# The second token tile's output projection: three fp32r matmuls on high and low parts instead of one fp32 matmul

## The chip, the cores and the metric

One core of a Trainium2 chip. The metric is the device time of one execution in microseconds, the median of three runs. The engines are TensorE (PE, with PEld for its weight loads), VectorE (DVE), ScalarE (ACT), GpSimd (POOL) and SyncE (SP), which issues the DMAs.

## The reference

Attention with keys and values pooled by 8, then two gated feed-forward layers over 2304 tokens, all fp32:

```python
# 4 batches, 8 heads, 576 tokens, head dimension 64: 2304 tokens of 512 columns
attn = softmax(scale * q @ mean8(k).T);  x = attn @ mean8(v)
# first layer, 512 -> 1536 -> 512
xn = x / rms * rms_g
g = xn @ w_gate
silu = g * (1.0 / (1.0 + np.exp(-g)))
val = xn @ w_val
x = silu * val @ w_out
# second layer, 512 -> 1536 -> 512
return (x @ w_a) * (x @ w_b) @ w_out2
```

## The kernel before

The first layer works on five tiles of tokens, `TILES1 = [512, 256, 512, 512, 512]` (line 20); the change concerns the second one, `idx == 1`, which has 256 tokens. The attention of later tokens is computed beside the matmuls of a tile: while tile 1 runs, the sub-tiles 6 to 9 of 128 tokens each pass through it, as the list `SIDE` (line 630) hands out their steps (`sub_steps`, line 287): scores (`sc`), maximum, exponent (`E`), transposition (`eP`, `eT`), values (`av`), normalization (`x`), sum of squares (`sq`, `ss`), a root per pair of sub-tiles (`root`, line 420, lines 427 to 441: `ba`, `br` and `by`, tensors of 128x2), the scaling of x (line 398) and its transposition (`xP`, line 405), from which the next tile's input is split into `xh` and `xl`.

For each of the twelve blocks f of 128 hidden columns a tile does this (loop from line 1106): gate and value projections (`project`, line 545), each 4 chunks x 3 matmuls, because an fp32 product is made of fp32r matmuls (a shortened fp32 format): low weights by high x, high by high, high by low. The parts of the weights are made anew for each tile by `split_w` (line 533): `wh` by a ScalarE cast, `wl` by a GpSimd subtraction, two buffers of each, so a block's parts are made when those of two blocks before are released. SiLU on ScalarE (line 1120) gives `ht`, VectorE multiplies it by the value (line 1127). Then the output projection of the block before it is added into four accumulators. In tiles 2 to 4 that is `out_proj` (line 562), 12 fp32r matmuls from `hh` and `hl`, the two parts of `ht` (lines 1136, 1137), and from `wh2` and `wl2`. In tiles 0 and 1 it is `out_direct` (line 573), 4 matmuls on fp32 `ht` and fp32 weights; the program issues each as two, so the profile shows 8 records per block. In tile 1 `ht` changes between two buffers, in tiles 2 to 4 it has one.

Tile 0 and all from the last tile on are ordered by hand. Tiles 1 to 3 are ordered by a scheduler when the program is built; each engine then works through its own list in that order, and an instruction that waits holds up all behind it on its engine.

Of the kernel before, what the change touches and what calls it, by code (L numbers as in the profile page):

```python
# [8 lines left out]
F32 = mybir.dt.float32  # L9
F32R = mybir.dt.float32r  # L10
# [7 lines left out]
P = 128  # L18
# [44 lines left out]
def attention_moe_moe2(  # L63
# [42 lines left out]
    h_p = first.enter_context(tc.tile_pool(name="h", bufs=2))  # L106
# [426 lines left out]
    def split_w(ph, f, i, part=None):  # L533
        if part != 1:
            wh = ws_p.tile([P, KD, P], F32R, tag=f"wh{i}", name=f"wh{i}")
            wl = ws_p.tile([P, KD, P], F32R, tag=f"wl{i}", name=f"wl{i}")
            nc.scalar.copy(wh, wf[ph, f, i])  # L537
            ws[i, f] = (wh, wl)
        if part != 0:
            wh, wl = ws[i, f]  # L540
            (nc.vector if boot["alt"] else nc.gpsimd).tensor_sub(  # L541
                wl, wf[ph, f, i], wh.bitcast(F32)
            )

    def project(tag, f, part, xs, cols, last, mid=None):
        xh, xl = xs
        wh, wl = ws.pop((part, f)) if last else ws[part, f]
        bank = ps.tile([P, 512], F32, tag=tag, name=tag)
        n = cols.stop - cols.start
        i = 0  # L550
        for c in range(KD):
            if c == 2 and mid is not None:
                mid()
            for w, x in ((wl, xh), (wh, xh), (wh, xl)):
                nc.tensor.matmul(  # L555
                    bank[:, :n], w[:, c, :], x[:, c, cols],
                    start=(i == 0), stop=(i == 3 * KD - 1),
                )
                i += 1
        return bank  # L560

    def out_proj(ph, f, accs, hs, cols, last):
        hh, hl = hs
        wh, wl = ws.pop((2, f)) if last else ws[2, f]
        n = cols.stop - cols.start
        for c in range(KD):
            for i, (w, x) in enumerate(((wl, hh), (wh, hh), (wh, hl))):
                nc.tensor.matmul(  # L568
                    accs[c][:, cols], w[:, c, :], x[:, :n],
                    start=(f == 0 and i == 0 and cols.start == 0), stop=(f == NF - 1 and i == 2),  # L570
                )

    def out_direct(f, accs, ht, cols):

        for c in range(KD):
            nc.tensor.matmul(  # L576
                accs[c][:, cols], wf[0, f, 2][:, c, :], ht[:, :cols.stop - cols.start],
                start=(f == 0 and cols.start == 0), stop=(f == NF - 1),
            )
# [65 lines left out]
    def new_accs():  # L645
        pairs = [ps.tile([P, 2, 512], F32, tag=f"acc{i}", name=f"acc{i}") for i in range(2)]
        return [pairs[c // 2][:, c % 2] for c in range(KD)]
# [432 lines left out]
    for idx, (ph, t0, n) in enumerate(work):  # L1080
        last_tile = idx + 1 == len(work)
        nxt = None if last_tile else work[idx + 1]
        side = SIDE[idx] if idx < len(SIDE) else []
        region = ExitStack()
        if last_tile:
            attn.close()
            side = second_front()
        if last_tile or idx == 0:
            region.enter_context(tc.manual_schedule(engines=set(HELD)))
        full = slice(0, n)  # L1090
        jobs = [(f, full, True, f + 1, True) for f in range(NF)]
        slot = {"n": 0, "done": 0}
        total = 4 * len(jobs)

        def step():
            slot["n"] += 1
            want = -(-len(side) * slot["n"] // total)
            while slot["done"] < want:
                side[slot["done"]]()
                slot["done"] += 1  # L1100

        accs = first_tile() if idx == 0 else new_accs()
        if idx == 0:
            jobs = []
        prev = None
        for f, cols, last, ahead, own in jobs:
            m = cols.stop - cols.start
            if ahead == NF:
                ahead = None if nxt is None else (nxt[0], 0)
            elif ahead is not None:  # L1110
                ahead = (ph, ahead)
            gb = project("g", f, 0, xs, cols, last)
            if ahead is not None:
                split_w(*ahead, 0)
            step()
            if idx == 1:
                ht = h_p.tile([P, 512], F32R, tag=("hh", "hl")[f % 2], name="ht").bitcast(F32)
            else:
                ht = h_p.tile([P, 512], F32, tag="ht", name="ht", bufs=1)
            nc.scalar.activation(out=ht[:, :m], in_=gb[:, :m], func=AF.Silu)  # L1120
            vb = project("v", f, 1, xs, cols, last, step)
            if ahead is not None:
                split_w(*ahead, 1)
            if own and idx > 1:
                split_w(ph, f, 2)
            step()
            nc.vector.tensor_mul(ht[:, :m], ht[:, :m], vb[:, :m])  # L1127
            if idx == 1:
                if prev is not None:
                    out_direct(prev[0], accs, *prev[1:3])  # L1130
                step()
                prev = (f, ht, cols, last)
                continue
            hh = h_p.tile([P, 512], F32R, tag="hh", name="hh")
            hl = h_p.tile([P, 512], F32R, tag="hl", name="hl")
            nc.scalar.copy(hh[:, :m], ht[:, :m])
            nc.vector.tensor_sub(hl[:, :m], ht[:, :m], hh.bitcast(F32)[:, :m])
            if prev is not None:
                out_proj(ph, prev[0], accs, *prev[1:])
            step()  # L1140
            prev = (f, (hh, hl), cols, last)
        if prev is not None and idx == 1:
            out_direct(prev[0], accs, *prev[1:3])
        elif prev is not None:
            out_proj(ph, prev[0], accs, *prev[1:])
        if nxt is not None:
            xs = XT[idx + 1]
        for c, acc in enumerate(accs):
            if last_tile:
                if c == 0:  # L1150
                    last_x = x_p.tile([P, KD, 512], F32R, tag="xh", name="last_x").bitcast(F32)
                ev = last_x[:, c]
            else:
                ev = ev_p.tile([P, 512], F32, tag="ev", name="ev")
            if c % 2 == 0:
                nc.scalar.copy(ev[:, :n], acc[:, :n])
            else:
                nc.vector.tensor_copy(ev[:, :n], acc[:, :n])
            nc.sync.dma_start(out=x2d[t0][c * P:(c + 1) * P, :], in_=ev[:, :n])
        region.close()  # L1160
# [60 lines left out]
```

## Time and profile before

| | |
|---|---|
| median of 3 runs | 994.43 us (994.41 to 997.38) |
| profiled execution | 994.85 us, span 992.9 us |
| busy: TensorE, VectorE, ScalarE, GpSimd | 960.8 (97%), 533.3 (54%), 448.2 (45%), 347.7 (35%) us |
| mean granted TensorE clock | 0.997 |
| tile 1 on TensorE | 169.10 to 243.21 us |

The span is the time from the first to the last instruction. Matmuls are pipelined: a record of a matmul is longer than its step to the next one, so lengths of work are taken from start to start. The granted clock is 1.00 at 2.4 GHz and 0.50 at 1.2 GHz.

### The profile page before, as it was taken

How to read it: one execution, taken by the hardware profiler on the slowest of the kernel's cores; microseconds unless marked ns; L12 is line 12 of the kernel's file. 1: busy time of each engine (PE TensorE's matmuls, PEld its weight loads, DVE VectorE, ACT ScalarE, POOL GpSimd, SP SyncE). 2: the span in 40 equal slices, each digit the busy share in tenths (PEclk: the TensorE clock that was granted, in tenths of full speed). 3: DMA queues.
4: the chain of work that ended last, by engine and by line, in shares of the span. 5: the costliest groups of instructions: out<-in, count | busy, mean ns of one | idle time of the engine just before them, and what ended most of it. 6: DMA issues, size and time to landing. Idle time of an engine off the chain costs nothing. (4 is left out here: it accounts for less than half of the span.)

```text
span 992.9 us, 13291 instructions
## 1 busy us (share of the span) xinstructions
PE 960.8 (97%) x4866; PEld 831.8 (84%) x4866; DVE 533.3 (54%) x875; ACT 448.2 (45%) x800; POOL 347.7 (35%) x293
## 2 busy tenths in 40 slices
PE   5889889999999999999999999999999999999998
PEld 4776556898888888888888899999999999888886
DVE  5799876433442424242158588777666665222321
ACT  4667353654635455453355455444343444321211
POOL 3424512443343444343475603344433333310000
PEclk9999999999999999999999999999999999999999
DMA  8565662000000010000120242444434435643431
GB/s 288 184 230 172 212 204 88 22 23 22 22 1 22 1 54 1 1 1 2 49 93 7 85 162 97 143 138 144 130 130 126 157 111 213 192 150 105 143 110 66
DMA packets 47776, 101.79 MB, mean 103 GB/s; under 512 B 5216, under 2 KB 19808, under 8 KB 47712
## 3 DMA queue, kind: packets, MB, share of 16 engines
q1 hardware_dynamic: 47568, 100.82, 31.2%
q8 instruction: 39, 0.64, 0.3%
q14 instruction: 25, 0.20, 0.1%
q10 hardware_dynamic: 144, 0.13, 0.0%
HBM read 74.19 MB, written 26.74 MB: 102 GB/s over the span
## 5 line engine op out<-in xcount | busy, mean ns | idle before, releaser
L541 POOL TENSOR_TENSOR wl<-wf,wh 128x512 fp32r<-128x512 f32 x142 | 189.4, 1341 | 269.9 <-ACT wh L537 266.4
L537 ACT CAST wh<-wf 128x512 fp32r<-128x512 f32 x156 | 94.5, 617 | 68.8 <-PE v L555 38.5
L1001 PE MATMUL o<-woh,hl 128*128 128x512 f32 x216 | 85.8, 397 | 0.0
L979 DVE TENSOR_TENSOR hl<-hf,hh 128x768 fp32r<-128x768 f32 x36 | 35.3, 986 | 93.5 <-ACT hh L978 93.4
L1001 PE MATMUL o<-woh,hh 128*128 128x512 f32 x216 | 85.0, 394 | 0.0
L1001 PE MATMUL o<-wol,hh 128*128 128x512 f32 x216 | 84.7, 392 | 0.0
L1127 DVE TENSOR_TENSOR ht<-ht,v 128x512 f32<-128x512 f32 (+1 forms) x48 | 29.6, 617 | 92.9 <-PE v L555 84.7
L555 PE MATMUL g<-xh,wl 128*128 128x512 f32 (+1 forms) x192 | 72.7, 379 | 0.0
L555 PE MATMUL v<-xh,wl 128*128 128x512 f32 (+1 forms) x192 | 71.9, 375 | 0.0
L555 PE MATMUL v<-xl,wh 128*128 128x512 f32 (+1 forms) x192 | 70.0, 364 | 0.0
L555 PE MATMUL v<-xh,wh 128*128 128x512 f32 (+1 forms) x192 | 69.9, 364 | 0.0
L555 PE MATMUL g<-xl,wh 128*128 128x512 f32 (+1 forms) x192 | 69.9, 364 | 0.0
L555 PE MATMUL g<-xh,wh 128*128 128x512 f32 (+1 forms) x192 | 69.7, 363 | 0.0
L576 PE MATMUL acc<-ht,wf 128*128 128x256 f32 (+1 forms) x208 | 69.4, 475 | 0.0
L978 ACT CAST hh<-hf 128x768 fp32r<-128x768 f32 x36 | 29.8, 834 | 87.2 <-PE o L1001 79.4
L513 POOL TENSOR_TENSOR w<-w,st 128x512 int32<-128x512 int32 x20 | 26.2, 1311 | 114.0 <-DVE w L506 112.9
L908 ACT COPY p<-X 128x384 f32<-128x384 f32 x36 | 17.3, 480 | 89.5 <-PE X L900 89.5
L568 PE MATMUL acc<-hh,wl 128*128 128x512 f32 x144 | 56.7, 394 | 0.0
L568 PE MATMUL acc<-hl,wh 128*128 128x512 f32 x144 | 56.4, 391 | 0.0
L568 PE MATMUL acc<-hh,wh 128*128 128x512 f32 x144 | 56.1, 389 | 0.0
L576 PEld LDWEIGHTS acc<-ht,wf 128*128 128x128 f32 x208 | 39.8, 198 | 19.0 <-issue 15.3
L1120 ACT ACTIVATE ht<-g 128x512 f32<-128x512 f32 (+1 forms) x48 | 26.1, 544 | 57.9 <-PE g L555 57.8
(197 smaller groups left out, 2511.6 us busy)
## 6 DMA issues: line engine op xcount, KB each, us to landing
hf<-h SPq DMA_DIRECT2D x36, 384.0 KB, 3.2
st<-in_moe_w_out_dram SPq DMA_DIRECT2D x24, 512.0 KB, 3.7
h<-u SPq DMA_DIRECT2D x36, 192.0 KB, 2.3
h<-p SPq DMA_DIRECT2D x36, 192.0 KB, 1.9
st<-in_moe_w_gate_dram SPq DMA_DIRECT2D x12, 512.0 KB, 3.7
st<-in_moe_w_val_dram SPq DMA_DIRECT2D x12, 512.0 KB, 4.1
st<-in_moe_w_a_dram SPq DMA_DIRECT2D x12, 512.0 KB, 4.4
st<-in_moe_w_b_dram SPq DMA_DIRECT2D x12, 512.0 KB, 3.4
```

The costliest lines, as they stand in the source:

```text
L513: (nc.vector if boot["alt"] else nc.gpsimd).tensor_tensor(out=bits, in0=bits, in1=low, op=ALU.add)
L537: nc.scalar.copy(wh, wf[ph, f, i])
L541: (nc.vector if boot["alt"] else nc.gpsimd).tensor_sub(wl, wf[ph, f, i], wh.bitcast(F32))
L555: nc.tensor.matmul(bank[:, :n], w[:, c, :], x[:, c, cols], start=(i == 0), stop=(i == 3 * KD - 1),)
L568: nc.tensor.matmul(accs[c][:, cols], w[:, c, :], x[:, :n], start=(f == 0 and i == 0 and cols.start == 0), stop=(f == NF - 1 and i == 2),)
L576: nc.tensor.matmul(accs[c][:, cols], wf[0, f, 2][:, c, :], ht[:, :cols.stop - cols.start], start=(f == 0 and cols.start == 0), stop=(f == ...
L908: nc.scalar.copy(t, src[:, :HALF])
L978: nc.scalar.copy(hh, hf)
L979: nc.vector.tensor_sub(hl, hf, hh.bitcast(F32))
L1001: nc.tensor.matmul(accs[i], x[:, sub], y, start=(f == 0 and j == 0), stop=(f == NF - 1 and j == 2),)
L1120: nc.scalar.activation(out=ht[:, :m], in_=gb[:, :m], func=AF.Silu)
L1127: nc.vector.tensor_mul(ht[:, :m], ht[:, :m], vb[:, :m])
```

## The change

Tile 1 is now treated as tiles 2 to 4: `ht` has one buffer, `split_w(ph, f, 2)` makes `wh2` and `wl2` for each block, a ScalarE cast makes `hh`, a VectorE subtraction `hl`, and `out_proj` does 12 fp32r matmuls of 256 columns where `out_direct` did 4 fp32 ones.

```diff
--- before.py
+++ after.py
@@ -1113,24 +1113,15 @@
             if ahead is not None:
                 split_w(*ahead, 0)
             step()
-            if idx == 1:
-                ht = h_p.tile([P, 512], F32R, tag=("hh", "hl")[f % 2], name="ht").bitcast(F32)
-            else:
-                ht = h_p.tile([P, 512], F32, tag="ht", name="ht", bufs=1)
+            ht = h_p.tile([P, 512], F32, tag="ht", name="ht", bufs=1)
             nc.scalar.activation(out=ht[:, :m], in_=gb[:, :m], func=AF.Silu)
             vb = project("v", f, 1, xs, cols, last, step)
             if ahead is not None:
                 split_w(*ahead, 1)
-            if own and idx > 1:
+            if own:
                 split_w(ph, f, 2)
             step()
             nc.vector.tensor_mul(ht[:, :m], ht[:, :m], vb[:, :m])
-            if idx == 1:
-                if prev is not None:
-                    out_direct(prev[0], accs, *prev[1:3])
-                step()
-                prev = (f, ht, cols, last)
-                continue
             hh = h_p.tile([P, 512], F32R, tag="hh", name="hh")
             hl = h_p.tile([P, 512], F32R, tag="hl", name="hl")
             nc.scalar.copy(hh[:, :m], ht[:, :m])
@@ -1139,9 +1130,7 @@
                 out_proj(ph, prev[0], accs, *prev[1:])
             step()
             prev = (f, (hh, hl), cols, last)
-        if prev is not None and idx == 1:
-            out_direct(prev[0], accs, *prev[1:3])
-        elif prev is not None:
+        if prev is not None:
             out_proj(ph, prev[0], accs, *prev[1:])
         if nxt is not None:
             xs = XT[idx + 1]
```

The scheduler orders all five engines anew within tile 1. Three places follow, all around the root of the first pair of sub-tiles (6 and 7), whose `x_6` and `x_7` are transposed in tile 1 for tile 2. `ht`, `hh` and `hl` carry a running number, `wl0`, `wl1` and `wl2` (`wh` likewise) are the parts of gate, value and output weights, and the third number in `wf0_0_5` is f.

VectorE's list before, from `x_7` over the multiplication of block f=3 to the first of the three rounds of the root (two more follow, and then line 398 twice):

```order
L382 TENSOR_TENSOR x_7_1567<-av_7_1552,rs_7_1564 128x512
L1127 TENSOR_TENSOR ht_1588<-ht_1588,v_1590 128x256
L427 TENSOR_SCALAR ba_6_1597<-ss_6_1489 128x2
L430 TENSOR_SCALAR br_6_1599<-ba_6_1597 128x2
L435 TENSOR_TENSOR by_6_1598<-br_6_1599 128x2
L436 TENSOR_TENSOR by_6_1598<-by_6_1598,ba_6_1597 128x2
L441 SCALAR_TENSOR_TENSOR br_6_1599<-by_6_1598,br_6_1599 128x2
```

The same stretch of VectorE's list now, with the same two rounds and line 398 behind it:

```order
L382 TENSOR_TENSOR x_7_1607<-av_7_1580,rs_7_1604 128x512
L1124 TENSOR_TENSOR ht_1628<-ht_1628,v_1630 128x256
L427 TENSOR_SCALAR ba_6_1637<-ss_6_1501 128x2
L430 TENSOR_SCALAR br_6_1639<-ba_6_1637 128x2
L1128 TENSOR_TENSOR hl_1673<-ht_1628,hh_1672 128x256
L435 TENSOR_TENSOR by_6_1638<-br_6_1639 128x2
L436 TENSOR_TENSOR by_6_1638<-by_6_1638,ba_6_1637 128x2
L441 SCALAR_TENSOR_TENSOR br_6_1639<-by_6_1638,br_6_1639 128x2
```

The subtraction `hl` of block f=3 has come in between `br` and the rounds; it waits for `hh` from ScalarE, and all below waits behind it.

GpSimd's list before, from the value weights of f=4 to the gate weights of f=7:

```order
L541 TENSOR_TENSOR wl1_1619<-wf1_0_4_678,wh1_1618 128x512
L541 TENSOR_TENSOR wl0_1649<-wf0_0_5_731,wh0_1648 128x512
L541 TENSOR_TENSOR wl1_1675<-wf1_0_5_747,wh1_1674 128x512
L541 TENSOR_TENSOR wl0_1703<-wf0_0_6_768,wh0_1702 128x512
L541 TENSOR_TENSOR wl1_1731<-wf1_0_6_800,wh1_1730 128x512
L541 TENSOR_TENSOR wl0_1759<-wf0_0_7_838,wh0_1758 128x512
```

GpSimd's list now, over the same stretch:

```order
L541 TENSOR_TENSOR wl1_1659<-wf1_0_4_678,wh1_1658 128x512
L541 TENSOR_TENSOR wl2_1663<-wf2_0_3_652,wh2_1662 128x512
L541 TENSOR_TENSOR wl0_1705<-wf0_0_5_731,wh0_1704 128x512
L541 TENSOR_TENSOR wl1_1731<-wf1_0_5_747,wh1_1730 128x512
L541 TENSOR_TENSOR wl2_1735<-wf2_0_4_690,wh2_1734 128x512
L541 TENSOR_TENSOR wl0_1775<-wf0_0_6_768,wh0_1774 128x512
L541 TENSOR_TENSOR wl1_1803<-wf1_0_6_800,wh1_1802 128x512
L541 TENSOR_TENSOR wl2_1807<-wf2_0_5_758,wh2_1806 128x512
L541 TENSOR_TENSOR wl0_1847<-wf0_0_7_838,wh0_1846 128x512
```

Behind each pair of gate and value parts now stands the `wl2` of the block before theirs, so three subtractions instead of two in a row.

ScalarE's list before, from the SiLU of f=3 to the value weights of f=6:

```order
L1120 ACTIVATE ht_1588<-g_1569 128x256
L537 CAST wh0_1648<-wf0_0_5_731 128x512
L537 CAST wh1_1674<-wf1_0_5_747 128x512
L390 ACTIVATE sq_7_1586,ss_6_1489<-x_7_1567 128x512
L1120 ACTIVATE ht_1654<-g_1635 128x256
L537 CAST wh0_1702<-wf0_0_6_768 128x512
L409 CAST xh_2_1632<-xP_6_1622 128x4x128
L537 CAST wh1_1730<-wf1_0_6_800 128x512
```

ScalarE's list now, over the same stretch:

```order
L1117 ACTIVATE ht_1628<-g_1609 128x256
L537 CAST wh0_1704<-wf0_0_5_731 128x512
L537 CAST wh1_1730<-wf1_0_5_747 128x512
L390 ACTIVATE sq_7_1626,ss_6_1501<-x_7_1607 128x512
L1127 CAST hh_1672<-ht_1628 128x256
L537 CAST wh2_1734<-wf2_0_4_690 128x512
L1117 ACTIVATE ht_1710<-g_1691 128x256
L537 CAST wh0_1774<-wf0_0_6_768 128x512
L537 CAST wh1_1802<-wf1_0_6_800 128x512
L409 CAST xh_2_1688<-xP_6_1666 128x4x128
L1127 CAST hh_1741<-ht_1710 128x256
```

`hh` of f=3 and `wh2` of f=4 have come in between the square `sq_7` and the SiLU of f=4 (`ht_1710`), which now has to wait for `hl` of f=3 as well, since there is one `ht` buffer; the weights of f=6 come behind that SiLU as before, now both ahead of the cast from `xP`.

## Rows read from the trace of the kernel before

**Rows 1.** Windows, tile 1 and after: length, busy (PE, PEld, DVE, ACT, POOL), clock, DMA.

```profile
169.10:243.21 74.11, 71.40 (x502) 66.70 (x501) 29.49 (x66) 40.15 (x68) 31.54 (x24) 1.00 0.08 29
243.21:576.00 332.79, 332.76 (x1590) 278.54 (x1589) 142.43 (x222) 161.35 (x274) 150.88 (x114) 1.00 0.10 31
```

**Rows 2.** The timeline of TensorE in tile 1: start, length, instruction, count.

```profile
201.24 0.28 PE L555 MATMUL v<-xh,wl 128*128 128x256 f32 x1
...
202.56 0.28 PE L555 MATMUL v<-xl,wh 128*128 128x256 f32 x1
202.68 1.89 PE L576 MATMUL acc<-ht,wf 128*128 128x256 f32 x8
204.22 0.47 PE L555 MATMUL g<-xh,wl 128*128 128x256 f32 x1
204.53 0.28 PE L555 MATMUL g<-xh,wh 128*128 128x256 f32 x1
```

**Rows 3.** TensorE's waits in tile 1: total, times, longest.

```profile
PE xP L405 <- DVE x L398: 2.2, 2, 1.1
PE sc L299 <- PE g L555: 0.4, 1, 0.4
```

**Rows 4.** Groups of tile 1: busy, mean ns; last row whole kernel, min/median/max ns.

```profile
L541 POOL TENSOR_TENSOR wl<-wf,wh 128x512 fp32r<-128x512 f32 x24 | 31.5, 1323 | 46.2 <-ACT wh L537 46.2
L537 ACT CAST wh<-wf 128x512 fp32r<-128x512 f32 x24 | 14.6, 617 | 7.6 <-PE v L555 7.6
L1127 DVE TENSOR_TENSOR ht<-ht,v 128x256 f32<-128x256 f32 x12 | 5.0, 417 | 16.1 <-PE v L555 9.2 <-ACT eT L351 3.7 <-ACT ht L1120 3.2
L1156 ACT COPY ev<-acc 128x256 f32<-128x256 f32 x1 | 0.4, 373 | 1.9 <-PE acc L576 1.9
...
L1137 DVE TENSOR_TENSOR hl<-ht,hh x36: 684/694/1856, 253.3 to 565.4; 128x512 fp32r<-128x512 f32 x36
```

**Rows 5.** The timeline of four engines in front of the first xP.

```profile
188.50 1.77 PE L369 MATMUL av<-VB,eT 128*128 128x130 f32 x12
...
190.73 2.62 POOL L541 TENSOR_TENSOR wl<-wf,wh 128x512 fp32r<-128x512 f32 x2 [4.47 <-ACT wh L537]
...
191.89 0.63 ACT L390 ACTIVATE sq<-x 128x512 bf16<-128x512 f32 x1
192.64 0.73 DVE L427 TENSOR_SCALAR ba<-ss 128x2 f32<-128x2 f32 x1 [0.84 <-ACT sq L390]
...
193.61 0.16 DVE L435 TENSOR_TENSOR by<-br 128x2 f32<-128x2 f32 x1
...
195.37 2.43 DVE L398 SCALAR_TENSOR_TENSOR x<-x,br,gain 128x512 f32<-128x512 f32 x2
195.44 1.81 POOL L541 TENSOR_TENSOR wl<-wf,wh 128x512 fp32r<-128x512 f32 x1 [2.10 <-ACT wh L537]
196.26 0.63 PE L405 MATMUL xP<-ident,x 128*128 128x128 f32 x4 [1.11 <-DVE x L398]
```

**Rows 6.** GpSimd and VectorE in tile 3; last row L436 in the whole kernel.

```profile
441.17 0.15 DVE L435 TENSOR_TENSOR by<-br 128x2 f32<-128x2 f32 x1
441.31 1.29 POOL L541 TENSOR_TENSOR wl<-wf,wh 128x512 fp32r<-128x512 f32 x1 [2.60 <-ACT wh L537]
441.35 1.27 DVE L436 TENSOR_TENSOR by<-by,ba 128x2 f32<-128x2 f32 x1
...
L436 DVE TENSOR_TENSOR by<-by,ba x24: 160/161/1269, 39.2 to 443.0; 128x2 f32<-128x2 f32 x24
```

**Rows 7.** TensorE in tile 0 around one gap; then a window (clock third last).

```profile
114.50 3.59 PE L576 MATMUL acc<-ht,wf 128*128 128x512 f32 x8
...
124.92 0.50 PE L670 MATMUL g<-xh,wl 128*128 128x512 f32 x1 [2.74 <-ACT ht L678]
...
126.62 5.07 PE L576 MATMUL acc<-ht,wf 128*128 128x512 f32 x8
...
126.00:128.00 2.00, 2.00 (x5) 1.15 (x4) 1.97 (x5) 2.00 (x5) 0.00 (x0) 0.54 0.40 152
```

## Prediction before the run

> **What bounds the kernel now.** I read the windows first, over the second tile (the 256-token one, 169.10 to 243.21 us) and the stretch after it. TensorE is busy 71.40 of 74.11 us there and 332.76 of 332.79 in the next stretch, both at the full clock [rows 1]; ScalarE (40.15), GpSimd (31.54) and VectorE (29.49) are each about half idle. The list of waits says that TensorE's few gaps in the tile are two waits of 1.1 us, where the transpose of x (xP) waits for VectorE's line 398, and one of 0.4 [rows 3]. So TensorE's work sets the end of the tile, after it TensorE runs without gaps, and what the tile gains or loses is carried on to the end. The timeline then gives the size of each piece, and the chain of small steps in front of xP, which is the one place where another engine is late.
>
> **What goes and what comes on TensorE.** A block of line 576 (4 fp32 matmuls, 8 records) starts at 202.68 and the next gate at 204.22: 1.54 us. The first gate matmul then takes 0.31 to the second, where the step between two reduced-precision (fp32r) matmuls of 256 columns is 0.12 (eleven steps from 201.24 to 202.56); that adds 0.19 [rows 2]. So 1.73 us per block. In its place stand 12 fp32r matmuls of the same shape as the projections, 12 x 0.12 = 1.44. The saving is 0.29 per block, 12 blocks: **-3.5 us**.
>
> The Trainium skill, FP8 and Floating Point Precision, section TensorE Precision Notes, says that true fp32 takes four passes through the array. As an estimate by that page, the fp32 block would take 16 x 0.12 = 1.92 and the saving would be 5.8 us; the trace has the block itself at 1.73, and that is used.
>
> **What is added elsewhere.** Per f-block: a wh2 cast on ScalarE (0.617), a wl2 subtraction on GpSimd (1.29 when nothing interferes, mean 1.32), a hh cast on ScalarE and a hl subtraction on VectorE [rows 4]. The trace has no hh or hl of 256 columns. For hh I take the 256-column copy, 0.37 (above it the 512-column cast of the weights, 0.62); for hl the 256-column multiplication, 0.42 (above it the 512-column hl, median 0.69). Twelve of each: ScalarE 40.15 + 11.9 = 52, GpSimd 31.5 + 15.5 = 47, VectorE 29.5 + 5 = 35 of some 75 us. No engine becomes the bound by its sum. Their results are due late: out_proj of block f stands behind gate and value of f+1 (2.9 us), and wl0 and wl1 are made two blocks ahead. Without that cover a wl2 would cost 0.62 + 1.29 per block; I count nothing. Tile 2 loses its first two wl2, which now serve this tile, and makes its own at the boundary; its first out_proj comes after the gates and values of two blocks of 512 columns, so nothing either. No transfer is added; the stores of the tile and the loads of q only follow TensorE.
>
> **What stands in the chain before xP.** This is the term that decides. Before: av starts at 188.50, ScalarE's square at 191.89, VectorE's ba at 192.64, nine small operations from 193.61 to 195.37 (1.76 us, 0.16 each with short steps), then line 398 twice in 2.43, and xP at 196.26 after a wait of 1.11 [rows 5]. Two things in it are GpSimd's: ba takes 0.73, to just behind the end of the GpSimd pair at 193.35, and the second line 398 is stretched while the wl from 195.44 takes 1.81. That these block each other is plain at 441.3: the small operation L436, 0.16 elsewhere, takes 1.27, exactly to the end of the wl that GpSimd began at 441.31, between two of VectorE's operations [rows 6].
>
> The Trainium skill, SBUF — State Buffer, section Who interferes with whom, says it as a rule: a VectorE instruction with two SBUF inputs shares a port with GpSimd, and the later one blocks for the whole instruction of the other. The trace agrees (1.27 against 0.16). By the rule, each wl that falls into the chain costs its 1.29; without it the change would gain about 3 us.
>
> After the change, with the order above, in the clock of before. TensorE: av ends at 189.9, five value matmuls, out_proj, gate and the whole value follow (0.68 + 3 x 1.44), so it arrives at xP at 194.9. VectorE: ba ends at about 193.5 as now. But wl2 of f=4 now stands in GpSimd's queue and is ready (wh2 at 193.2), so it runs from 193.5 to 194.8 and br waits for it. Then comes hl of f=3 (0.42, to 195.4), which stands in VectorE's queue ahead of the small operations. There is one ht buffer now, so this hl releases the next SiLU (195.45); wh0 follows, and GpSimd starts wl0 of f=6 at about 196.5 and wl1 behind it, while VectorE needs 1.76 us for the small operations, to 197.2. Both wl cut in between two of them: 2 x 1.29, small operations done at 199.7, line 398 0.75, xP at 200.5. The wait is 5.6 us; if wl2 misses the chain, 4.3. I take 4.9, that is **+3.8** over the 1.11 of now.
>
> The second pair of sub-tiles has the same chain. With T the end of its av, TensorE arrives at T + 5.2 (11 gate matmuls, value, out_proj, 8 of the next gate). The square waits for x and ends by T + 2.2 to 2.8; then ba, br, nine small operations, the next multiplication, hl of f=10 and line 398 take 3.8 us undisturbed. GpSimd brings the rest of wl2 (0.6), wl0 and wl1 of tile 2's first block and wl2 of f=11 (1.29 each): xP at T + 9 to T + 11, a wait of 3.9 to 5.8. I take 4.6, **+3.5** over now.
>
> **The clock.** A TensorE gap of 2.74 us before 124.92 was followed by a granted clock of 0.54 in 126 to 128 us (mostly the 1.2 GHz level, not 2.4), and the fp32 block there took 5.07 against 3.59 for the same block at 114.50 [rows 7]: 1.5 us. The two 1.1 us gaps of the tile cost no clock [rows 1]. Gaps of over 4 us should, so 2 x 1.5 = **+3.0**; bounds 0 and 2 x 1.8.
>
> **Small waits.** av waits 0.2 us for eT in two places because hh and wh2 stand ahead of it on ScalarE, the last out_proj waits 0.25 to 0.9 for hl of f=11, and the 0.4 us wait goes: **+0.4**, between -0.2 and +2 (the upper end if one transpose of E is late as well).
>
> Sum: -3.5 + 3.8 + 3.5 + 3.0 + 0.4 = **+7.2 us**. The profiled execution took 994.85 (span 992.9), 0.42 above the median of 994.43, so 1002.05 beside it, **1001.6** beside the median. All lower bounds at once (+3.2, +2.8, 0, -0.2) make +2.3, all upper ones (+4.5, +4.7, +3.6, +2) +11.3; short of that, this case reaches from 998 to 1005.
>
> **Rivals.**
> 1. *The lock does not bite, the saving comes through.* The chain of now has two of these conflicts and still costs only 1.1 us, and over the kernel hl and L436 mostly run undisturbed (medians 0.69 and 0.16) [rows 4, 6]. Then the chains run free: xP at about 196.5 and T + 6, waits of 1.6 and 0.8, no clock loss: -3.5 + 0.5 - 0.3 + 0.3 = -3.0, **991.4**. Against it: GpSimd is busy 47 of 75 us, and the SiLU released by hl puts two wl straight into the chain. It decides if at most one wl per chain falls behind the point where TensorE arrives anyway.
> 2. *One wl per chain.* If ScalarE delivers wh0 and wh1 later than I walk it, or VectorE keeps the port over its run of small operations, each chain is only 1.29 longer than free: waits of 2.8 and 2.1, +1.7 and +1.0. With +0.6 for the rest that is -0.2, and 1.5 more if the clock falls once: **994.2 to 995.7**. For it: in the later tiles, where wl2 exists already, the chain is rarely cut as in rows 6. Against it: there a block is 512 columns wide, so the same three wl come half as densely.
> 3. *It runs away.* Each late multiplication makes the next hh, hl and SiLU late, and the transposes of E wait too (1.2 us each): another 3 to 4 us, **1005**.
> 4. *The matmuls are not cheaper.* The new matmuls have the shape, the types and the weight loads of the tile's projections, which run at the step of 0.12 [rows 2], so I give this no chance of its own.
>
> **Chances.** Forecast 0.56, rival 1 0.13, rival 2 0.24, rival 3 0.07. A measurement of this kernel can tell about 0.3% (3 us) from no change. Faster than 991.45: half of rival 1 and a little, 0.08. Within: the other half, nearly all of rival 2 and the low edge of the forecast, 0.31. Slower than 997.4: 0.61. For 8 in 10 the range runs from 992 to 1004.5; the forecast's own is 998 to 1005.
>
> **What would show it.** In the changed profile: the step from out_proj to the next gate 1.44 instead of 1.73; two waits of xP for line 398 of 4 to 5.6 us; VectorE operations of 128x2 with over 1 us, each ending with a wl of GpSimd; a granted clock near 0.5 for some 3 us after each; the tile's stretch at about 81 us instead of 74.1, and the stretches behind it unchanged to 0.5 us. The forecast is wrong if the waits stay under 2 us or if the clock holds through them; the saving is wrong if the tile's stretch without these waits is not 3 to 4 us shorter.

## The result, and the profile after

The kernel after takes 1005.0 us (median of 6 runs, 1002.5 to 1005.7) beside 995.75 for the kernel before (6 runs, 994.4 to 997.4). The ratio is 1.0086, with a 95% interval of 1.0072 to 1.0100: slower by 8.6 us by that ratio, 9.25 between the medians. Single executions of either kernel spread over 3 us; the profiled ones are 1002.46 and 994.85, their spans 1000.4 and 992.9, 7.5 apart. The windows of the kernel after, the second tile and then a stretch behind it with as many matmuls as that of [rows 1] (same columns):

```profile
169.14:251.36 82.22, 71.98 (x550) 69.98 (x549) 45.08 (x78) 49.74 (x91) 45.91 (x35) 0.94 0.09 27
251.36:584.00 332.64, 332.64 (x1590) 278.49 (x1589) 142.49 (x223) 161.99 (x275) 152.15 (x115) 1.00 0.10 32
```

The tile starts where it started (169.14 against 169.10) and is 8.1 us longer (82.22 against 74.11). Behind it TensorE has no gaps, as before; from the next tile's first gate matmul to the first matmul of line 900 it takes 325.72 us, in the kernel before 325.96. So the whole loss of the profiled execution arises in the tile. TensorE's waits in it, in the kernel after:

```profile
PE xP L405 <- DVE x L398: 8.4, 2, 4.3
PE sc L299 <- issue: 1.0, 1, 1.0
PE acc L568 <- DVE hl L1128: 0.8, 1, 0.8
```

They add up to 10.2 us where [rows 3] had 2.6. The other part is in the busy time: 71.98 is a little more than before's 71.40, although the new matmuls are the cheaper ones. The timeline of TensorE shows both halves of that, first an undisturbed block of the new projection, then one behind the first long wait:

```profile
190.83 0.28 PE L568 MATMUL acc<-hh,wl 128*128 128x256 f32 x1
...
192.26 0.28 PE L555 MATMUL g<-xh,wl 128*128 128x256 f32 x1
...
199.64 1.08 PE L405 MATMUL xP<-ident,x 128*128 128x128 f32 x4 [4.34 <-DVE x L398]
...
201.16 0.41 PE L568 MATMUL acc<-hh,wl 128*128 128x256 f32 x1
201.37 0.41 PE L568 MATMUL acc<-hh,wh 128*128 128x256 f32 x1
```

From 190.83 to 192.26 the block takes 1.43, where the fp32 block of [rows 2] took 1.73. Behind the wait of 4.34 the step is 0.21 instead of 0.12. The windows of the kernel after behind it give the granted clock (third column from the end): half, and then a mean of half and full. Around the second wait it is 0.60 from 240 to 242 us, while TensorE still stands, 0.50 from 242 to 246 and 0.70 from 246 to 248.

```profile
200.00:202.00 2.00, 2.00 (x11) 2.00 (x10) 1.11 (x4) 0.89 (x2) 0.00 (x0) 0.50 0.00 0
202.00:204.00 2.00, 2.00 (x16) 2.00 (x15) 0.40 (x2) 0.77 (x2) 0.07 (x1) 0.79 0.00 0
```

Why x is late is in the rows of VectorE, GpSimd and ScalarE in front of the first xP of the kernel after; they answer to [rows 5]:

```profile
190.80 3.79 POOL L541 TENSOR_TENSOR wl<-wf,wh 128x512 fp32r<-128x512 f32 x3 [1.66 <-ACT wh L537]
...
193.41 1.22 DVE L430 TENSOR_SCALAR br<-ba 128x2 int32<-128x2 int32 x1
194.53 0.42 DVE L1128 TENSOR_TENSOR hl<-ht,hh 128x256 fp32r<-128x256 f32 x1
195.04 0.38 ACT L1117 ACTIVATE ht<-g 128x256 f32<-128x256 f32 x1 [1.90 <-DVE by L435]
...
196.01 2.48 POOL L541 TENSOR_TENSOR wl<-wf,wh 128x512 fp32r<-128x512 f32 x2 [1.42 <-ACT wh L537]
196.03 1.25 DVE L435 TENSOR_TENSOR by<-br 128x2 f32<-128x2 f32 x1
197.32 1.19 DVE L436 TENSOR_TENSOR by<-by,ba 128x2 f32<-128x2 f32 x1
...
198.74 1.42 DVE L398 SCALAR_TENSOR_TENSOR x<-x,br,gain 128x512 f32<-128x512 f32 x2
```

GpSimd now runs three subtractions from 190.80 to 194.59, where before ran two to 193.35. `br`, 128 rows of two numbers, takes 1.22 and ends with the third, which is the new `wl2`. Then `hl` is done, SiLU starts at 195.04 (the row names a small `by` operation as what it waited for; with one `ht` buffer it can't start before `hl` has read it), and behind it come two more subtractions at 196.01. The two small operations that meet them take 1.25 and 1.19 instead of 0.16. In front of the second xP the same stands once more:

```profile
236.23 2.54 POOL L541 TENSOR_TENSOR wl<-wf,wh 128x512 fp32r<-128x512 f32 x2 [0.25 <-ACT wh L537]
236.25 1.30 DVE L435 TENSOR_TENSOR by<-br 128x2 f32<-128x2 f32 x1
237.58 1.21 DVE L436 TENSOR_TENSOR by<-by,ba 128x2 f32<-128x2 f32 x1
...
242.51 1.08 PE L405 MATMUL xP<-ident,x 128*128 128x128 f32 x4 [4.07 <-DVE x L398]
```

So it is the chain that is longer. From the last values of a pair (`av`) to its first xP the kernel after takes 11.07 and 11.04 us, the kernel before 7.77 and 7.89; TensorE arrives at xP 6.73 and 6.96 us behind the start of that `av`, nearly as in the kernel before (6.66 and 6.77).

### The profile page after: what moved, and what is told of

It is laid out like the page before. It is cut to its first block, busy times and chain, and to the rows that moved or that the text cites. A ratio compares the mean times of both kernels' runs of the same rounds, so it can differ in the third digit from the quotient of the medians.

```text
span 1000.4 us, 13463 instructions
## 1 busy us (share of the span) xinstructions
PE 960.6 (96%) x4914; PEld 835.2 (83%) x4914; DVE 548.6 (55%) x887; ACT 458.7 (46%) x824; POOL 363.0 (36%) x305
## 5 line engine op out<-in xcount | busy, mean ns | idle before, releaser
L541 POOL TENSOR_TENSOR wl<-wf,wh 128x512 fp32r<-128x512 f32 x154 | 205.0, 1340 | 264.1 <-ACT wh L537 260.2
L537 ACT CAST wh<-wf 128x512 fp32r<-128x512 f32 x168 | 101.8, 618 | 70.8 <-PE v L555 35.8
L568 PE MATMUL acc<-hl,wh 128*128 128x512 f32 (+1 forms) x192 | 70.5, 367 | 0.8 <-DVE hl L1128 0.8
L568 PE MATMUL acc<-hh,wl 128*128 128x512 f32 (+1 forms) x192 | 71.0, 370 | 0.0
L568 PE MATMUL acc<-hh,wh 128*128 128x512 f32 (+1 forms) x192 | 70.1, 365 | 0.0
L1128 DVE TENSOR_TENSOR hl<-ht,hh 128x512 fp32r<-128x512 f32 (+1 forms) x48 | 45.3, 945 | 30.9 <-ACT hh L1127 30.7
L1001 PEld LDWEIGHTS o<-woh,hh 128*128 128x128 f32 x216 | 40.5, 188 | 10.2
```

The source lines that it names most:

```text
L541: (nc.vector if boot["alt"] else nc.gpsimd).tensor_sub(wl, wf[ph, f, i], wh.bitcast(F32))
L568: nc.tensor.matmul(accs[c][:, cols], w[:, c, :], x[:, :n], start=(f == 0 and i == 0 and cols.start == 0), stop=(f == NF - 1 and i == 2),)
L1001: nc.tensor.matmul(accs[i], x[:, sub], y, start=(f == 0 and j == 0), stop=(f == NF - 1 and j == 2),)
```

## The experiments

The theory to test: TensorE stands in front of a late attention chain, made late by GpSimd's subtractions, and the clock falls behind each long wait; the matmuls themselves are cheaper. Rivals are the other side work (ScalarE's copies, `hl`, the one `ht` buffer), the matmul form, and a tile that is bound by side work as a whole. "Stretch" is the second tile from its first gate matmul to the next tile's; before has 74.11, after 82.22. Stretches are those of one profiled execution each; each time is set beside runs of the kernel before on the same chip. The pieces of code are shortened: arguments that don't matter here, and lines around them, are left out.

### 1. The short matmuls without the side work, the side work without them, and all but GpSimd's part

The first run has the short matmuls on operands that exist anyway:

```
-  nc.tensor.matmul(accs[c][:, cols], wf[0, f, 2][:, c, :], ht[:, :n])
+  for i, w in enumerate((wl, wh, wh)):          # wh, wl: parts of the value weights
+      nc.tensor.matmul(accs[c][:, cols], w[:, c, :], hr[:, :n])   # hr: product written as fp32r
```

> The kernel before, with the second tile's output projection issued as 12 matmuls of 128x256 on fp32r operands a block, but with none of the new side work: the weights are the high and low parts of the value weights that lie in SBUF already, and the hidden values are the VectorE product written as fp32r, used for all terms (so the projection's values are left out). GpSimd, ScalarE and VectorE have the kernel before's work. THEORY (the matmuls save 0.29 us a block, and all of the loss comes from side work that lengthens the two waits for xP): 12 x 0.29 = 3.5 us faster than before, about 992 us (ratio 0.9965), the waits for xP near the 1.1 us of before, the tile's stretch near 74.1 - 3.5 = 70.6 us. RIVAL A (the fp32r form itself costs, through weight loads or the order that it brings): 994.5 to 997 or more. RIVAL B (shorter blocks make PE arrive earlier at a chain that is no shorter, so that the saving goes into longer waits): the xP waits grow to some 2 to 3 us in all beyond before and the time stays within 2 us of before.

Measured: 997.77 (10 runs), ratio 1.0019 (1.0009 to 1.0028). Not faster at all. Window of the tile, and TensorE's longest waits in it, in this run:

```profile
170.48:245.74 75.26, 69.16 (x550) 67.76 (x549) 31.32 (x66) 39.26 (x67) 29.34 (x23) 0.98 0.09 29
```

```profile
PE xP L405 <- DVE x L398: 5.3, 2, 3.0
```

The time and the waits (3.1 us more than before's 2.2) are rival B's, but not its mechanism. TensorE does not come earlier: it arrives at xP 6.62 and 6.72 us behind the start of the pair's last `av`, as in the kernel before. The chain is longer: 9.62 and 9.01 us. VectorE and GpSimd in front of the first xP of this run:

```profile
195.57 1.29 POOL L541 TENSOR_TENSOR wl<-wf,wh 128x512 fp32r<-128x512 f32 x1 [0.36 <-ACT wh L537]
195.68 1.21 DVE L436 TENSOR_TENSOR by<-by,ba 128x2 f32<-128x2 f32 x1
...
198.23 1.26 POOL L541 TENSOR_TENSOR wl<-wf,wh 128x512 fp32r<-128x512 f32 x1 [1.37 <-ACT wh L537]
198.31 1.20 DVE L441 SCALAR_TENSOR_TENSOR br<-by,br 128x2 f32<-128x2 f32 x1
```

Two of GpSimd's old subtractions now fall among the small operations of each chain; in the kernel before, the one that came next started at 195.44, behind them [rows 5]. One clock drop (0.50 in 202 to 204 us) adds 1.0 us of busy time. The run is not the matmuls alone, though. The scheduler ordered the tile anew (the last `av` of the first pair stands behind 96 gate and value matmuls instead of 88), and the stand-in weights are held until the output projection has read them, so that casts on ScalarE wait for it (2.98 us at 193.23). What it shows is that the saving can be lost without any added work on the other engines, by where their old work falls.

The second run keeps the side work and the fp32 matmuls:

```
-  out_proj(ph, prev[0], accs, *prev[1:])
+  out_direct(prev[0], accs, prev[1][0].bitcast(F32), prev[2])      # prev[1][0]: hh
```

> The kernel after, with its side work (high and low parts of the output weights and of the hidden values in the second tile), but with the projection done by 4 fp32 matmuls a block from the fp32 weights and the high part (the low parts are computed and not read). THEORY (the side work costs the two long waits and the clock drops behind them, and the matmuls save 3.5 us): slower than after by 3.5 us less the 0.8 us wait for hl that goes: 1005 + 3.5 - 0.8 = about 1007.5 us, waits for xP of 3 to 5 us each. RIVAL A (the matmul form costs, the side work doesn't): 994 to 998 us, waits as before. RIVAL B (longer blocks make PE arrive later, so that the waits are shorter by what the blocks are longer): 1003 to 1005 us.

Measured: 1007.0 (4 runs), ratio 1.0108 (1.0090 to 1.0126), close to the expected number and for another reason. The tile is only 77.31 long; but it starts at 178.31 instead of 169.10. Nothing reads `wh2` and `wl2` here, so nothing holds them back, and the scheduler put them into the first tile. The experiment with the same work less `wl2` comes below; TensorE's order in the second tile is the same as here.

The third run leaves out `wl2` alone:

```
+  if own and idx == 1:
+      nc.scalar.copy(wh, wf[ph, f, 2]);  ws[2, f] = (wh, wh)
```

> The kernel after without the second tile's subtraction for the low part of the output weights on GpSimd (the high part stands in for it, so the term wl x hh is left out); all matmuls, the copies on ScalarE and the subtraction hl on VectorE stay. THEORY (the waits come from GpSimd's subtractions, which hold up VectorE's two-column root operations; one third of them is new): GpSimd goes back to 2 subtractions a block, the waits for xP fall from 4.3 and 4.1 us to 1 to 2.5 us each, at least one clock drop goes (1.5 to 2 us): 997 to 1001 us. RIVAL (the load on ScalarE and VectorE, or the single buffer of the hidden tile, lengthens the chain): waits stay at 4 us, 1003 to 1005 us.

Measured: 997.18 (10 runs), ratio 1.0008 (0.9996 to 1.0021). Window of the tile and longest waits in it, in this run:

```profile
167.97:246.50 78.53, 71.14 (x551) 69.23 (x549) 42.26 (x78) 49.87 (x91) 32.43 (x25) 0.96 0.08 28
```

```profile
PE xP L405 <- DVE x L398: 5.6, 2, 3.3
```

The twelve subtractions are worth 3.7 us of the tile; TensorE, VectorE and ScalarE work through the tile in the order of the kernel after. In the medians they are worth more: 8.6 us above the kernel before became 0.8 (single executions of this run go from 994.8 to 999.5, the profiled one took 998.12). The waits fell less than expected, 5.6 us remain. Here too it is GpSimd, with its old load:

```profile
193.78 2.48 POOL L541 TENSOR_TENSOR wl<-wf,wh 128x512 fp32r<-128x512 f32 x2 [1.62 <-ACT wh L537]
193.80 1.26 DVE L435 TENSOR_TENSOR by<-br 128x2 f32<-128x2 f32 x1
```

The next small operation takes 1.18 under the second of the two, and in the other chain two take 1.15 and 1.00 (at 234.00 and 235.41). So the third subtraction is one part of the loss, and the place to which the new order brings the old two is another.

### 2. GpSimd alone

The first try failed. It added one subtraction a block that reads only the loaded weights:

```
+  nc.gpsimd.tensor_sub(spare, wf[ph, f, 2], wf[ph, f, 2])     # kernel before, idx == 1
```

> The kernel before with one subtraction of 128x512 more on GpSimd a block in the second tile, which nobody reads (12 in all, 1.3 us each); matmuls, PE's order and the other engines' work as before. THEORY (a running GpSimd subtraction holds up VectorE's root operations, so the chain before xP gets longer by what GpSimd is busier): the two xP waits grow from 1.1 us to 2 to 4 us each, with one or two clock drops of 1.5 to 2 us: stretch 76 to 80 us against 74.1, 997 to 1002 us. RIVAL (GpSimd is off the path; 15 us more of it in 74 cost nothing): waits and stretch as before, 994.4 to 997.3 us.

Measured: 999.85 (4 runs), ratio 1.0046 (1.0030 to 1.0062), as expected in size; but the group of these subtractions shows where they ran (durations in ns, then first and last start):

```profile
L1126 POOL TENSOR_TENSOR wl<-wf x12: 1042/1156/1484, 24.3 to 164.5; 128x512 fp32r<-128x512 f32 x12
```

All twelve are in the first tile; the second starts at 173.93 instead of 169.10 and is 74.09 long, untouched. This says nothing on the theory. The second try ties the subtraction to a part that ScalarE writes in the same block:

```
+  nc.gpsimd.tensor_sub(spare, wf[ph, f, 2], ws[1, ahead[1]][0].bitcast(F32))
```

> The kernel before with one more GpSimd subtraction of 128x512 a block in the second tile, which nobody reads, this time taken from a high part that ScalarE writes in that block, so that it can't be moved into the first tile as in the run before. Matmuls, PE's order and the other engines' work as before. THEORY (a running GpSimd subtraction holds up VectorE's root operations): second tile 1.5 to 4 us longer than before's 74.1, its xP waits 1.5 to 3.5 us each; 997 to 1000 us. RIVAL (GpSimd is off the path; what cost 3.7 us in the kernel after is the order or ScalarE's copy): 74.1 us and 1.1 us each, 994.4 to 997.3 us.

Measured: 1000.27 (4 runs), ratio 1.0047 (1.0034 to 1.0061). Window, waits, and VectorE and GpSimd in front of the first xP of this run:

```profile
166.82:248.13 81.31, 74.25 (x502) 69.44 (x501) 32.00 (x66) 40.15 (x68) 47.48 (x37) 0.96 0.08 27
```

```profile
PE xP L405 <- DVE x L398: 6.6, 2, 3.3
```

```profile
188.46 2.62 POOL L541 TENSOR_TENSOR wl<-wf,wh 128x512 fp32r<-128x512 f32 x2 [3.23 <-ACT wh L537]
188.48 0.69 DVE L382 TENSOR_TENSOR x<-av,rs 128x512 f32<-128x512 f32 x1
189.12 0.42 DVE L1130 TENSOR_TENSOR ht<-ht,v 128x256 f32<-128x256 f32 x1
190.40 0.72 DVE L427 TENSOR_SCALAR ba<-ss 128x2 f32<-128x2 f32 x1 [0.86 <-ACT sq L390]
191.05 1.30 POOL L1126 TENSOR_TENSOR wl<-wf,wh 128x512 fp32r<-128x512 f32 x1
191.15 1.22 DVE L430 TENSOR_SCALAR br<-ba 128x2 int32<-128x2 int32 x1
...
193.17 1.26 POOL L541 TENSOR_TENSOR wl<-wf,wh 128x512 fp32r<-128x512 f32 x1 [0.83 <-ACT wh L537]
193.19 1.26 DVE L436 TENSOR_TENSOR by<-by,ba 128x2 f32<-128x2 f32 x1
```

This settles the theory's main point. TensorE, ScalarE and VectorE have the same instructions in the same order as in the kernel before, and nobody waits for the added subtractions. The tile is 7.2 us longer: 4.4 more waiting for xP (6.6 against 2.2) and 2.85 more busy time (74.25 against 71.40), which is the half clock behind both waits. `br` ends with the added subtraction (192.37 and 192.35), `L436` with the next one. The waits, 3.3 us each, lie in the expected 1.5 to 3.5; the stretch came out above the expected 1.5 to 4 us, because no clock drop had been counted. In the medians the run is 4.3 us slower than before, less than its tile. Two of GpSimd's old subtractions moved along (14 in the first tile and 26 in the second, where before has 16 and 24), and in the profiled execution the first tile is 2.3 us shorter (the second starts at 166.82 instead of 169.10). So the 7.2 us are the price, in the tile, of 13 more subtractions: 11 of the twelve new ones and the two that moved.

### 3. The copies and hl alone

The second run of above without `wl2`, so that only ScalarE's copies and `hl` are added:

```
-  split_w(ph, f, 2)
+  split_w(ph, f, 2, 0)          # high part only, idx == 1
```

> The kernel before with the other three added operations a block in the second tile: the weights' high part and the hidden high part on ScalarE, the hidden low part on VectorE through the single hidden buffer; no subtraction for low weights, and the projection by fp32 matmuls from the high part (the low parts left out). THEORY (GpSimd's subtraction is the larger half of the side work's cost): stretch 74.5 to 76.5 us, 995 to 998 us, waits for xP under 2 us each. RIVAL (ScalarE's and VectorE's share, and SiLU waiting for the hidden buffer, is the larger one): stretch 76.5 to 78 us, near the 77.3 us of the run with all of the side work.

Measured: 996.16 (10 runs), ratio 1.0006 (0.9993 to 1.0019), stretch 75.91: the theory's case. The waits for xP are 1.9 us each, and the clock stays up. (`wh2` is read by nobody here and was made in the first tile, so this is the price of `hh`, `hl` and the one `ht` buffer.) So the tile pays 1.2 us in the run with the short matmuls, 1.8 in that with `hh` and `hl`, 7.2 in that with a third subtraction a block, and 8.1 with all of them. That is less than their sum. The first two runs have orders of their own, and the clock drops of two of the runs can be paid only once; which of this makes the difference isn't shown.

### 4. Taking the chain off TensorE's path

The first attempt sets the second tile's attention steps into slots of TensorE's own order, with xP later:

```
+  SIDE[1] = placed()      # 48 slots; scores 0, turn 3, values 5 | 7, 10, 12 | xP 20, 22 | next pair + 24
+  tc.manual_schedule(engines={PE})   # second tile only
```

> The kernel after, with the second tile's attention steps set in slots of PE's program order: root chain started behind the second sub-tile's values as now, but the transposes of x come 8 and 10 quarter-blocks (about 11.5 and 14.5 us) later instead of about 5 us. No work is added or left out. THEORY (the loss is PE standing in front of a late chain, and the clock drops behind it): both waits for xP (8.4 us) and the 3.5 us of half clock go, some 0.2 to 1 us stays in small waits: 1005 - 8.4 - 3.5 = about 993 us (991 to 996), faster than before by about 2 us. RIVAL A (lost throughput, not a late chain: PE's blocks themselves wait for ScalarE, VectorE or GpSimd): the waits turn up at g, v or acc, 1000 to 1005 us. RIVAL B (the later xP holds the one attention bank and delays the next scores, and the next tile waits for its inputs): waits at sc and at the start of the next tile of some us, 996 to 1001 us.

Measured: 1001.41 (5 runs), ratio 1.0042 (1.0023 to 1.0061), stretch 79.75. The first xP no longer waits for line 398, but TensorE's waits in the tile are now these:

```profile
PE eP L346 <- ACT E L339: 6.1, 4, 2.7
PE xP L405 <- DVE xl L413: 3.1, 2, 1.5
```

None of the three cases had named the largest of these waits: my three slots are too short for the exponentials. The other is the bank of rival B: the second xP of a pair needs the one attention bank, which the low part of the first is still reading. The placement was poor, so the run doesn't price the late chain. The next order gives the exponentials five slots and lets the third sub-tile's scores, turns and values run while the root of the first two is computed:

```
+  for s, k, j in ((6, 0, 0), (7, 8, 1), (8, 16, 0), (9, 28, 1)):  # scores k, turn k+5, values k+7
+  for s, k in ((6, 24), (7, 26), (8, 43), (9, 45)):               # xP
```

> The kernel after, with PE's order in the second tile written by slots: the third sub-tile's scores, turns and values run while the root chain of the first two is under way, exponentials get 5 slots instead of 3, and the transposes of x stand 9 and 11 slots behind the values that they need. All work is done as in the kernel after. THEORY (the tile is set by the serial attention chain through the one attention bank and not by PE's own work, so what PE saves turns into waiting unless the chain is laid beside other work): waits in the tile fall from 10.3 us to 0.5 to 3 us and the clock stays up, so the saving of the matmuls shows: tile stretch 68 to 71 us against 82.2, time 990 to 994 us, faster than before. RIVAL (side work on ScalarE, VectorE and GpSimd, busy 50 us of the tile each, sets the blocks themselves): waits move to g, v or acc, stretch 75 us or more, 996 us or more.

> The same slots for PE's order in the second tile, on the kernel before (fp32 matmuls, no new side work). THEORY: the waits of before (2.6 us in this tile) nearly go: stretch about 71.5 to 73 us, 993 to 995 us; and the same order on the kernel after is faster than this one by the 12 x 0.29 = 3.5 us of the matmuls, less what small waits the side work still costs (0 to 1.5 us). RIVAL (the matmuls' saving is not real when measured end to end): both orders give the same time within 1 us.

> The overlapped order with the 12 short matmuls a block but none of the new side work (high and low parts of the value weights and a hidden product in fp32r stand in, so the projection's values are left out). THEORY (the matmuls do save 12 x 0.29 = 3.5 us, which only shows where PE does not wait for the attention chain): 3 to 3.5 us faster than the overlapped order on the kernel before (993.1), so 989.5 to 990.5 us, where the same matmuls in the old order gained nothing. RIVAL (shorter blocks meet the next late step): 991.5 to 993.5 us, with the missing time in waits for eP, av or xP.

Measured, each against the kernel before in its old order: on the kernel after 994.55 (11 runs), ratio 0.9985 (0.9974 to 0.9997); on the kernel before 993.06 (11 runs), 0.9976 (0.9966 to 0.9986); with the short matmuls alone 989.79 (4 runs), 0.9938 (0.9923 to 0.9954). The windows of the tile for the kernel before and for the matmuls alone:

```profile
168.66:240.03 71.37, 70.05 (x502) 66.74 (x501) 28.99 (x66) 39.72 (x68) 30.75 (x24) 1.00 0.09 30
```

```profile
171.63:240.06 68.43, 66.81 (x550) 66.01 (x549) 30.41 (x66) 39.57 (x67) 29.59 (x23) 1.00 0.10 32
```

Here, where TensorE waits 1.3 and 1.6 us in all, the matmuls' saving shows: 3.24 us of busy time, 2.9 of the stretch, 3.5 in the medians beside before (6.2 us below it on one chip, 2.7 on another). The same matmuls in the scheduler's order had gained nothing. The complete kernel after does not get it, though: it was expected to be the faster of the two in this order by 2 to 3.5 us and is 1.5 slower. Its TensorE and VectorE at the place of the longest wait:

```profile
204.10 0.39 PE L568 MATMUL acc<-hl,wh 128*128 128x256 f32 x1 [1.79 <-DVE hl L1149]
```

```profile
200.12 2.52 DVE L398 SCALAR_TENSOR_TENSOR x<-x,br,gain 128x512 f32<-128x512 f32 x2
202.56 1.48 DVE L1149 TENSOR_TENSOR hl<-ht,hh 128x256 fp32r<-128x256 f32 x1
```

`hl` stands behind both scalings and is itself stretched, and the clock falls behind the wait (0.50 in 206 to 208). Two attempts to mend that: the matmuls that read `hl` last in a block, with the scalings one and two slots later; and, with the scalings as they were, `wl2` on VectorE.

```
+  terms.sort(key=lambda t: t[1] == 2)                  # both
+  at[k + 8] += [SUB[s - 1]["scale"]];  at[k + 9] += [u["scale"]]     # first
+  boot["alt"] = idx == 1                               # second: VectorE in split_w
```

> The overlapped order on the kernel after, with two changes: in the second tile the eight matmuls that don't need the hidden low part stand before the four that do, and the two scalings of x are issued one and two slots later than the root chain instead of at once. In the overlapped run PE stood 1.8 us in front of a low part that was queued on VectorE behind the two scalings (2.5 us), and the clock fell behind that. THEORY (side work costs only where PE meets a late low part): the 1.8 us, the clock drop of about 2 us and most of the 0.8 us before the last block's low part go: 3 to 4.5 us off 994.6, so 990 to 992 us, about 2 us faster than the same order on the kernel before (993.1). RIVAL (another piece of side work is late next, at silu or at the transposes of x): 993 to 995 us.

> The overlapped order on the kernel after, with the second tile's matmuls that need the hidden low part last in a block (scalings of x at once, as in the first overlapped run), and with the second tile's subtraction for low output weights on VectorE instead of GpSimd. No work is left out. THEORY (what is left of the loss is GpSimd's third subtraction a block, which holds VectorE up; without it the matmuls' 3 us show): GpSimd's busy time in the tile falls from 44 to about 31 us, VectorE's rises by some 12 x 0.7 = 8 us less what it no longer waits; stretch 69 to 71 us, 990 to 992 us, faster than the same order on the kernel before (993.1). RIVAL (the operation itself, on whichever engine, makes the low parts late): waits for hl and x stay at 2 to 4 us in all, 993 to 995 us.

Measured: 993.65 (8 runs), ratio 0.9978 (0.9967 to 0.9990), and 995.46 (12 runs), 1.0003 (0.9989 to 1.0018). The first is the rival's case; the second came out above even that (993 to 995). TensorE's longest waits in the tile, first of the one, then of the other:

```profile
PE xP L405 <- DVE x L382: 2.0, 1, 2.0
PE acc L571 <- DVE hl L1154: 1.1, 1, 1.1
```

```profile
PE xP L405 <- DVE x L382: 1.6, 1, 1.6
PE v L555 <- DVE ht L1150: 1.3, 1, 1.3
PE xP L405 <- DVE xl L413: 1.3, 1, 1.3
```

With `wl2` on VectorE, GpSimd is back to 24 full subtractions in the tile, but now `x`, `ht` and `xl` of VectorE are late; all waits come to 7.3 us. Beside the same order on the kernel before, the side work costs about what the matmuls save with `wl2` on GpSimd, and more with it on VectorE. In the profiled executions the tile of the kernel after in the new order is not shorter than before's 74.1 (75.1 in the first such run, 0.7 of it the next tile's first gate matmuls, which TensorE takes ahead of the last block), so I don't claim that the small gains of 0.15 and 0.22% come from the tile. What beats both kernels is the order, not the form: the overlapped order on the kernel before, by 0.24% (0.14 to 0.34). On the kernel after, with `hl` last, it stands beside that within the intervals, not in front of it.

## Why the prediction was right

The forecast was 1001.6, the result 1005.0: slower, as forecast, at the upper edge of the forecast's own range (998 to 1005) and 0.5 us above the 8-in-10 range (992 to 1004.5). Of the 3.4 us, 1.3 are the starting point, since the kernel before has 995.75 by six runs and not 994.43. In the profiled tile the loss is 8.1 where 7.2 was forecast. The steps:

- **The saving, -3.5.** The block came out at 1.43 instead of 1.73, as said, and the run with the overlapped order has 3.24 us less busy time by it. Rival 4 is refuted by that. The prediction's own sign for it, a stretch that is 3 to 4 us shorter without the waits for xP, did not come: 73.8 against 71.9. That sign left out the half clock, which the sum counts; without it and the small waits 68.2 stand against 71.4.
- **The chains, +3.8 and +3.5.** Measured 4.34 and 4.07 against 1.1 each: +6.2 in all, 1.1 less than forecast. The walk through the first chain held step by step: `br` waits for `wl2`, `hl` stands ahead of the small operations, its end releases SiLU and by that two more subtractions, which cut in between two small operations (at 195.45 and 196.5 in the forecast, 195.04 and 196.01 in the trace). xP came at 199.64, between the two variants of 199.2 and 200.5.
- **The clock, +3.0.** Half clock came with both waits. Busy time is 71.98, where 71.40 - 3.24 = 68.2 was due: +3.8. The windows of the granted clock give nearly the same by themselves: what is lost of it while TensorE works is 1.6 us behind the first wait and 2.3 behind the second, the longer drop.
- **Small waits, +0.4.** They were 1.8 us (0.8 for `hl` of the last block, 1.0 at a scores matmul) against 0.4: +1.4. The 0.8 was foreseen, the 1.0 was not; that matmul starts at 223.42, right behind the end of line 382 at 223.32, in front of which `hl` had taken 1.29 instead of 0.42 on VectorE (the row names no releaser).

Sum by the trace: -3.2 + 6.2 + 3.8 + 1.4 = 8.2, measured 8.1. It closes because the 3.8 is what the saving leaves of the busy time; the clock's windows are the check on it. The terms that were too small, clock and small waits, outweigh the one that was too large, so the total is nearer than its parts. The stretch behind the tile is unchanged to 0.24 us, as forecast. The two profiled executions are 7.6 apart, the medians 9.25; no trace shows where the rest lies.

Rival 1 (no lock) is excluded by the run with the subtraction alone, which lengthens the tile by 7.2. Rival 2 (one subtraction a chain) is excluded by the rows: in the first chain two more follow the `wl2` that held `br`, in the second two hold the small operations. Rival 3 gave 1005, which is the time that came, but not its mechanism: no transpose of E waits in the tile, and xP's waits are not longer than forecast.

One reading behind the sum was too simple. The prediction counted the saving as sure, and the chains as what the new side work might make of them. The run with the short matmuls and no new side work shows that the saving is not sure either: 5.3 us of waits with GpSimd's old load, where rival 1 had counted 2.4 with the new. Nor is the third subtraction a block all of the price: without it, in the same order, the chains are still cut twice each by the old two. The prediction saw this in its walk, where `hl` releases SiLU and by that `wl0` and `wl1`; its account of what is added elsewhere counts only the new work.

What stays open: how much of the waits the single `ht` buffer brings. The run with `hh` and `hl` has that buffer too and lost 1.8 us, but without the third subtraction; a second buffer was not tried. Filling the waits with idle matmuls to hold the clock was not tried either.

## What to carry to other kernels

A busy share of 96% does not make work taken off an engine a gain: see how early its next operand is ready, and where the new order puts the other engines' work in front of that operand. Before work is added to an engine that has time, look at what that engine holds up while it runs; here GpSimd subtractions that nobody waited for made the tile 7.2 us longer and the whole run 4.3. An added operation that nothing reads is not a fair test of a cost, because a scheduler moves it to where it is free to run; tie it to something made at the place in question.

## What was not expected of the hardware

- Not only operations with two operands in SBUF were held up by a GpSimd subtraction: `br` and `ba`, with one, took 1.22 and 0.72 (0.17 undisturbed) and ended with it. Operations with one operand in PSUM, where the matmuls' results lie, ran at their usual 0.69 and 0.42 beside a running subtraction (188.48 and 189.12 in the run with GpSimd alone).
- The same wait was followed by a clock drop or not. In the two runs with the same order of the second tile, TensorE waited 1.88 and 1.89 us for the first xP; these are windows behind the wait, of the first and of the second:

```profile
208.00:210.00 2.00, 2.00 (x6) 1.58 (x5) 2.00 (x3) 0.82 (x2) 1.27 (x1) 0.50 0.01 4
```

```profile
196.00:198.00 2.00, 2.00 (x13) 1.79 (x13) 1.42 (x3) 1.33 (x3) 0.15 (x1) 1.00 0.00 0
```

Within the first of these runs the second xP waited 1.88 us as well, and the clock held. In the second tiles of all runs it held with every wait of up to 1.57 us, fell with every one of 2.70 us and more, and did either in between (with 2.26 it fell, with 2.29 it held). That is no bound: in the first tile of the run without `wl2` it held at 1.00 behind a wait of 3.18 us, at 123.34.
